# A hand-drawn issue order drawn anew: gated linear attention followed by a SoLU feed-forward block

## The chip, the core and the metric

The kernel runs on one NeuronCore of one Trainium2 chip. The metric is the device time of one execution in microseconds. The engines are called PE (TensorE matmul), PEld (its weight loads), DVE (VectorE), ACT (ScalarE), POOL (GpSimd) and SP (SyncE, whose queue issues most DMAs). Each engine works off its own queue in the order in which the program issues to it, so an instruction that waits holds up those behind it on its engine.

## The reference, cut to what matters

```python
# attention: q, k, v, alpha are (4, 8, 768, 48) float32, alpha in 0.8 .. 1.0
for t in range(S):
    state = alpha[:, :, t, :, None] * state + einsum('bhd,bhe->bhde', k[:, :, t], v[:, :, t])
    y[:, :, t] = einsum('bhd,bhde->bhe', q[:, :, t], state)
x = y.transpose(0, 2, 1, 3).reshape(3072, 384)
# feed-forward: w_in (384, 1024), w_out (1024, 384), both float64 in memory, g_ln (1024)
h = x @ w_in
solu = h * softmax(h)
ln = (solu - mean(solu)) / sqrt(var(solu) + 1e-6) * g_ln
out = ln @ w_out
```

## The kernel before, in words

**Tiling.** The 768 steps of a sequence are cut into G = 6 groups of 128. In a group all 4 batches and 8 heads are handled together: the batch gives a quarter of the 128 partitions. The output is made in N = 24 products of 128 tokens; product m belongs to group m // 4 and batch m % 4. "Product" below means the feed-forward work on 128 tokens.

**Attention of one group** is a chain over several engines:
- `load` (SP) brings alpha, k and q of a group into the tiles `an`, `kn`, `qn`, `load_v` brings v into `vn`. For group 0 `load_first` does it by token, and `turned` transposes on PE with `ends` copied by ACT first.
- `alpha_T` and `alpha_max` (DVE) transpose alpha and take its largest value.
- `scan_back(g, i)` (L179, DVE, a scan of 128x516, three thirds i) gives the decay hT; `keys_T` (L159 and L160, DVE transposes) and `keys` (L201, POOL) give the decayed keys kT; `decay` (L222, L225, POOL) decays the state.
- `scan_on(g, i)` (L189 to L193 and L179, DVE: copy, maximum, reciprocal, scan) gives the forward products in aT; `queries_T` (L159, L160) and `queries` (L213, L215, POOL) give the decayed queries qv; `apart` (L208, ACT) spreads the last columns of the queries by parity.
- `keys_back(g)` transposes kT on PE (L258) into PSUM banks, and ACT copies it to `kg` (L260).
- `scores(g, half)` (L239, PE, 64 instructions a half) fills four PSUM banks, and `masked(half)` (L250, DVE) multiplies them by the triangle mask into sT, which empties the banks.
- `read_begin`, `read_state` and `read_values` (L271, PE) make y; ACT copies it to xT (L296); `next_state` (L308 PE, L317 DVE) adds the group's state.

The four PSUM banks with the tags a0 to a3 are shared by the transposed keys, the scores, y and the state's product. Whoever comes next waits until the one before has been read.

**The feed-forward block of product m.** `up(m, half)`: 24 matmul instructions (L329) into one of two banks h, then on ACT e = exp(h) (L334), on DVE u = h e (L335), on ACT u squared (L336). The bank is free when u is made. `partial(m)` adds e on POOL and u squared on DVE over the eight column blocks (L344, L347, L349). `down(m, half)` is the product with w_out (L358), with two small sums (L364) at the end. `finish(m)` works out the scale (L373 to L380 DVE, `r` L384 POOL), ACT writes o_sb (L386), SP stores it (L388). The scale can only be made after the product is done, and o_sb frees one of two banks o.

**Conversion of the weights.** w_in and w_out come as float64 in 14 pieces: 0 to 5 are w_in (512 columns), 6 to 13 are w_out (384 columns). `fetch(i)` (L421, SP) loads a piece into one of four buffers `raw`; `bits(i)` (L437 to L444, four DVE instructions) splits it into `top` and `low`; `add(i)` adds the two on PE (L457, a product with the identity into a bank o) and ACT copies the sum into the weight (L461, L459); `in_range(i)` (L471, L474, ACT) tests the range and is the last reader of the buffer. `centre` subtracts the mean from w_out (L492 to L501), once all pieces are there.

**What sets the order.** The schedule is manual: the engines receive their instructions in the order of the calls at the end of the function. Ahead of the loop these calls are written out one by one: first the start, group 0 and products 0 to 3 with the conversions among them, then group 1 with the downs of products 0 to 3. In the loop over m from 4 to 24, product m rises (`up`), product m - 1 falls (`down`), product m - 2 is finished, and beside them the four steps s = 0 to 3 of group g = m // 4 + 1 are done, for g = 2 to 5.

Of the kernel before, what the change touches and what calls it, by code (L numbers as in the profile page):

```python
# [16 lines left out]
P = 128  # L17
# [15 lines left out]
def fast_path(ctx, tc, q, k, v, alpha, moe_w_in, moe_w_out, moe_g_ln, out):  # L33
# [104 lines left out]
    def turned(src, out):  # L138

        x = by_token(src)  # L140
        ends = two.tile([P, B, H * E1], FP, tag="two", name="ends")
        nc.scalar.copy(out=ends.rearrange("p b (h d) -> p b h d", h=H), in_=x[:, :, :, E0:D])
# [14 lines left out]
    def blocks(src, dst, extra):  # L157

        nc.vector.transpose(out=dst.rearrange("p h (t u) -> p h u t", u=TQ), in_=src[:, :, :, 0:E0])  # L159
        nc.vector.transpose(  # L160
            out=extra.rearrange("p j (i t u) -> p u j i t", u=TQ, i=2),
            in_=src[:, :, :, E0:D].rearrange("p (j i) u d -> p u j i d", i=2),
        )

# [38 lines left out]
    def queries_T(g):  # L203
        blocks(qn, qv[:, 0:H], qe)
# [7 lines left out]
    def queries(g):  # L212
        nc.gpsimd.tensor_tensor(out=qe, in0=qe, in1=aT[:, H:NB, 1:SW], op=ALU.mult)  # L213
        apart()
        nc.gpsimd.tensor_tensor(out=qv[:, 0:H], in0=qv[:, 0:H], in1=aT[:, 0:H, 1:SW], op=ALU.mult)  # L215
# [212 lines left out]

    def bits(i):
# [15 lines left out]
        made[i] = low, top.bitcast(FP)  # L445

# [15 lines left out]

    def in_range(i):


        if not float64:
            return
        F = words(i)[0].shape[1]
        raw = raws.pop(i)
        sq = work.tile([P, 512], FP, name="sq")[:, 0:F]  # L470
        nc.scalar.activation(  # L471
            out=sq, in_=raw[:, 0:F, 1].bitcast(FP), func=AF.Square, accum_out=far[:, i, 0:1]
        )
        nc.scalar.activation(out=sq, in_=sq, func=AF.Exp, scale=-(2.0**24), accum_out=far[:, i, 1:2])  # L474

    def convert(i):
        bits(i)
        add(i)
        in_range(i)
# [28 lines left out]

    nc.scalar.dma_start(out=ident, in_=inline(np.eye(P), "ident_c"))
    for i in range(3):  # L510
        fetch(i)
    load_first(alpha, an)
# [3 lines left out]
    nc.scalar.dma_start(out=g_rows, in_=moe_g_ln.rearrange("(c p) -> c p", p=P))  # L516
    load_first(k, kn)
    load_first(q, qn)
    nc.gpsimd.memset(unit, 0.0)
    nc.gpsimd.memset(unit[:, :, 0:1], 1.0)  # L520
    nc.gpsimd.memset(vn, 0.0)
# [8 lines left out]
    load_v(0)  # L530
    fetch(3)

    for i in range(3):
        bits(i)
        add(i)
    alpha_max(0)
    t = banks("tp_a", [NP, P], 3)
    turned(an, t)
    for i in range(3):
        nc.scalar.copy(out=aT[:, NP * i : NP * i + NP, 1:SW], in_=t[i])  # L540
    for i in range(3):
        in_range(i)
        fetch(i + 4)
        scan_back(0, i)
    t = [ps_h.tile([P, NP, P], FP, tag="h", name=f"tp_k{i}") for i in range(2)]
    t.append(ps_a.tile([P, NP, P], FP, tag="a3", name="tp_k2"))
    turned(kn, t)
# [4 lines left out]
    turned(qn, t)  # L552
# [10 lines left out]
    bits(3)  # L563
    masked(0)
    scores(0, 1)
    add(3)
    masked(1)
    bits(4)
    read_begin()
    read_values(0)  # L570
    add(4)
    for i in (3, 4):
        in_range(i)
        fetch(i + 4)
    load(alpha, an, 1)


    up(0, 0)
    up(1, 0)
    bits(5)  # L580
    add(5)
    keys_back(0)
    next_state(0)
    in_range(5)
    fetch(9)
    load(k, kn, 1)
    up(0, 1)
    convert(6)
    fetch(10)
    up(1, 1)  # L590
    partial(0)
    convert(7)
    fetch(11)
    partial(1)
    convert(8)
    fetch(12)
    up(2, 0)
    convert(9)
    fetch(13)
    load(q, qn, 1)  # L600
    load_v(1)
    up(2, 1)
    partial(2)
    convert(10)
    convert(11)
    up(3, 0)
    convert(12)
    convert(13)
    up(3, 1)
    centre()  # L610
# [3 lines left out]
    for i in range(3):  # L614
        scan_back(1, i)
    decay(1)
    down(0, 0)
    down(0, 1)
    keys_T(1)
    keys(1)  # L620
    finish(0)
    for i in range(3):
        scan_on(1, i)
    down(1, 0)
    down(1, 1)
    queries_T(1)
# [557 lines left out]
```

## Time and profile before

| | us |
|---|---|
| median of three runs | 556.03 (553.51 to 556.2) |
| the profiled execution's own time | 554.89 |
| its span, first to last instruction | 553.0 |
| PE busy | 435.9 (79%) |
| DVE busy | 273.3 (49%) |
| POOL busy | 140.6 (25%) |
| ACT busy | 130.5 (24%) |
| mean granted PE clock | 0.883 of full |

The page of the profile also follows the chain of work that ended last, from the last instruction back. By engine it reads:

```profile
PE 55%; DVE 28%; issue 5%; ACT 5%; POOL 3%; DMA 2%; SPq 0%; DVEq 0%; ACTq 0%
```

PE holds a little over half of the chain and DVE more than a quarter: the end is set by PE and DVE in turns. The groups of instructions show the largest shares of PE; the columns are busy time, mean ns of one instruction, and the idle time before them with its releaser:

```profile
L329 PE MATMUL h<-xT,w_in 128*128 128x128 f32 x1152 | 138.4, 280 | 0.0
L358 PE MATMUL o<-w_out,u 128*128 128x385 f32 x384 | 134.5, 500 | 1.1 <-DVE w_out L501 0.6
L239 PE MATMUL a<-qv,kT 32*128 32x128 f32 x768 | 51.6, 396 | 55.5 <-POOL qv L215 34.1
```

A mean of one instruction is longer than its share of the time, since matmuls overlap. Busy shares are averages over stages with different limits, so a change is read from its own stage.

### The profile page before, as it was taken

To read this page: it belongs to the slowest core of one execution; us is meant where nothing else is said; L and a number is where in the kernel's file an instruction comes from. 1 tells how busy PE (TensorE), PEld (TensorE's weight loads), DVE (VectorE), ACT (ScalarE), POOL (GpSimd) and SP (SyncE) were. 2 spreads that over 40 slices of the span, in tenths; PEclk is the share of its full clock that TensorE was granted. 3 is DMA by queue.
4 is the path that set the end of the run, shared out by engine and by line. 5 is a ranking of instruction groups with operands and counts; after the bars stand their busy time and mean duration, and the time that the engine had idled before them with its cause. 6 is when DMAs were issued, how large, how long until landed. Compare 5 with 4: busy or idle time off the path is not lost.

```text
span 553.0 us, 12123 instructions
## 1 busy us (share of the span) xinstructions
PE 435.9 (79%) x5365; PEld 345.1 (62%) x5365; DVE 273.3 (49%) x483; ACT 130.5 (24%) x252; POOL 140.6 (25%) x148
## 2 busy tenths in 40 slices
PE   4769755478669598389995699994899948999993
PEld 1558543345447496367884577884589736888772
DVE  4583335444973338444477245583542873313431
ACT  1603423233020032111222212231122221223220
POOL 3000021201420026222064302362220832202430
PEclk9878887879886899579998789996899988999997
DMA  6970441530003564012235130415213100000001
GB/s 161 177 160 6 113 112 57 99 45 0 0 30 78 110 101 88 0 32 43 41 48 107 22 72 19 58 32 112 58 32 44 31 15 0 17 18 15 14 17 49
DMA packets 85118, 30.90 MB, mean 56 GB/s; under 512 B 64568, under 2 KB 83264, under 8 KB 85056
## 3 DMA queue, kind: packets, MB, share of 16 engines
q1 hardware_dynamic: 84608, 29.90, 26.4%
q8 instruction: 44, 0.72, 0.6%
q10 hardware_dynamic: 448, 0.14, 0.1%
q14 instruction: 18, 0.15, 0.1%
HBM read 25.30 MB, written 4.72 MB: 54 GB/s over the span
## 4 chain that ended last, share of the span: by engine, by line
PE 55%; DVE 28%; issue 5%; ACT 5%; POOL 3%; DMA 2%; SPq 0%; DVEq 0%; ACTq 0%
PE h L329 18%; PE o L358 11%; PE a L239 8%; PE y L271 8%; PE sum L457 6%; DVE aT L179 3%; DVE hT L179 3%; DVE u L335 2%; DVE part_u L344 2%; DVE part_u L347 2%; ACT e L334 2%; ACT u L336 2%; DVE qv L159 2%; DVE kT L159 2%; DVE sT L250 2%
## 5 line engine op out<-in xcount | busy, mean ns | idle before, releaser
L329 PE MATMUL h<-xT,w_in 128*128 128x128 f32 x1152 | 138.4, 280 | 0.0
L329 PEld LDWEIGHTS h<-xT,w_in 128*128 128x128 f32 x1152 | 134.9, 196 | 5.1 <-issue 4.1
L358 PE MATMUL o<-w_out,u 128*128 128x385 f32 x384 | 134.5, 500 | 1.1 <-DVE w_out L501 0.6
L335 DVE TENSOR_TENSOR u<-h,e 128x512 f32<-128x512 f32 x48 | 33.2, 691 | 170.4 <-ACT e L334 170.4
L344 POOL TENSOR_TENSOR part_e<-e 128x512 f32<-128x512 f32 x24 | 30.6, 1273 | 292.3 <-ACT e L334 292.3
L358 PEld LDWEIGHTS o<-w_out,u 128*128 128x128 f32 x384 | 72.0, 194 | 49.0 <-issue 4.9
L239 PE MATMUL a<-qv,kT 32*128 32x128 f32 x768 | 51.6, 396 | 55.5 <-POOL qv L215 34.1
L239 PEld LDWEIGHTS a<-qv,kT 32*128 32x128 f32 x768 | 46.0, 294 | 61.8 <-POOL qv L215 34.8
L334 ACT ACTIVATE e<-h 128x512 f32<-128x512 f32 x48 | 28.5, 593 | 102.7 <-PE h L329 102.6
L457 PE MATMUL sum<-low,ident 128*128 128x384 f32 (+1 forms) x28 | 21.3, 858 | 35.4 <-DVE low L444 35.4
L336 ACT ACTIVATE u<-u 128x512 f32<-128x512 f32 x48 | 30.2, 630 | 48.7 <-DVE u L335 48.7
L250 DVE TENSOR_TENSOR sT<-a,mask 128x512 f32<-128x512 f32 x48 | 29.7, 680 | 21.3 <-PE a L239 21.3
L386 ACT ACTIVATE o_sb<-o,r 128x384 f32<-128x384 f32 x24 | 14.0, 582 | 109.7 <-POOL r L384 109.7
L457 PEld LDWEIGHTS sum<-low,ident 128*128 128x128 f32 x28 | 6.3, 265 | 41.1 <-DVE low L444 23.3
L384 POOL TENSOR_TENSOR r<-sums,mhalf 128x1 f32<-128x1 f32 x24 | 15.8, 660 | 54.7 <-DVE sums L380 54.6
L347 POOL TENSOR_TENSOR part_e<-part_e 128x256 f32<-128x256 f32 x24 | 28.3, 1181 | 1.9
L344 DVE TENSOR_TENSOR part_u<-u 128x512 f32<-128x512 f32 x24 | 19.0, 793 | 14.6 <-ACT u L336 14.6
L271 PE MATMUL y<-sT,vn 128*32 128x128 f32 x768 | 24.4, 290 | 0.0
L271 PE MATMUL y<-qv,state 32*32 32x128 f32 x1280 | 19.1, 281 | 5.8 <-issue 5.8
L271 PEld LDWEIGHTS y<-sT,vn 128*32 128x32 f32 x768 | 22.5, 118 | 1.5 <-issue 1.1
L296 ACT COPY xT<-y 128x384 f32<-128x384 f32 x24 | 11.5, 479 | 46.6 <-PE y L271 46.6
L179 DVE TENSOR_TENSOR_SCAN aT<-aT,seed 128x516 f32<-128x516 f32 x18 | 22.2, 1232 | 0.6
(101 smaller groups left out, 437.7 us busy)
## 6 DMA issues: line engine op xcount, KB each, us to landing
an<-in_alpha_dram SPq DMA_DIRECT2D x24, 192.0 KB, 4.1
kn<-in_k_dram SPq DMA_DIRECT2D x24, 192.0 KB, 5.0
qn<-in_q_dram SPq DMA_DIRECT2D x24, 192.0 KB, 4.5
out_dram<-o_sb SPq DMA_DIRECT2D x24, 192.0 KB, 1.9
vn<-in_v_dram SPq DMA_DIRECT2D x24, 128.0 KB, 3.4
raw<-in_moe_w_out_dram SPq DMA_DIRECT2D x8, 384.0 KB, 3.9
raw<-in_moe_w_in_dram SPq DMA_DIRECT2D x16, 128.0 KB, 3.2
vn<-in_v_dram SPq DMA_DIRECT2D x24, 64.0 KB, 3.1
```

Of the source, the lines that this page charges most:

```text
L179: nc.vector.tensor_tensor_scan(out=o, data0=a, data1=s, initial=1.0, op0=ALU.mult, op1=ALU.add)
L239: nc.tensor.matmul(a[b][:, i], lhsT=kT[quarter(b), kb], rhs=qv[quarter(b), qb], start=kb == h, stop=kb != h, tile_position=(32 * b, 0), sk ...
L250: nc.vector.tensor_tensor(out=sT[:, b, half * NP : half * NP + NP], in0=a[b], in1=mask[:, None, :].to_broadcast([P, NP, P]), op=ALU.mult,)
L271: nc.tensor.matmul(reading["y"][b][quarter(r), a], lhsT=lhsT, rhs=rhs, start=(b, r) not in begun, stop=stop, tile_position=(row, 32 * r), ...
L329: nc.tensor.matmul(h[:, f], lhsT=w_in[:, a, (f0 + f) * P : (f0 + f + 1) * P], rhs=d["xT"][:, a], start=(a == 0), stop=(a == KC - 1),)
L334: nc.scalar.activation(out=d["e"][:, fs], in_=h, func=AF.Exp)
L335: nc.vector.tensor_tensor(out=d["u"][:, fs], in0=h, in1=d["e"][:, fs], op=ALU.mult)
L336: nc.scalar.activation(out=d["u2"][:, fs], in_=d["u"][:, fs], func=AF.Square)
L344: eng.tensor_tensor(out=t, in0=d[key][:, 0:HF], in1=d[key][:, HF:FC], op=ALU.add)
L347: eng.tensor_tensor(out=t[:, 0:w], in0=t[:, 0:w], in1=t[:, w : 2 * w], op=ALU.add)
L358: nc.tensor.matmul(o[:, 0 : DM + 1], lhsT=d["u"][:, f], rhs=w_out[:, f], start=(f == 0), stop=(f == FC - 1), skip_group_check=True,)
L457: nc.tensor.matmul(src, lhsT=ident, rhs=x, start=k == 0, stop=k == 1)
```

## The change

The computation is the same; every instruction of the function is still there. What differs is the order of the calls, and with it the order on each engine. Line numbers after the change are some lines higher (L179 becomes L186, L258 becomes L264).

- **Start.** Alpha is fetched ahead of the weights, keys and queries ahead of piece 2. The copy `ends` is taken out of `turned` and issued earlier. The sums of pieces 0 to 2, which stood ahead of group 0, are spread among its steps.
- **Conversions.** `in_range(i)` is issued with `bits(i)`, and `fetch(i + 4)` right behind it. Each `bits(i)` stands one product ahead of its `add(i)`.
- **Group 1.** Keys and the forward scans come before `down(0)` is finished, `apart` behind `finish(1)`, the first scores between the halves of `down(3)`; the loads of group 2 are spread.
- **Loop.** Two of the three backward scans move up to the step's start, keys come before the decay, two of the three forward scans move into step 0. In step 1 the last scan and the queries come between the halves of `up`, and the smaller query transpose comes first. In step 2 both halves of the scores come later: the first behind the whole `up`, the second behind the whole `down`.

```diff
-    def turned(src, out):
+    def ends_of(src):
+        ends = two.tile([P, B, H * E1], FP, tag="two", name="ends")
+        nc.scalar.copy(out=ends.rearrange("p b (h d) -> p b h d", h=H), in_=by_token(src)[:, :, :, E0:D])
+        return ends
+
+    def turned(src, ends, out):
...
     def queries_T(g):
-        blocks(qn, qv[:, 0:H], qe)
+        blocks(qn, qv[:, 0:H], qe, True)
...
     def queries(g):
         nc.gpsimd.tensor_tensor(out=qe, in0=qe, in1=aT[:, H:NB, 1:SW], op=ALU.mult)
-        apart()
         nc.gpsimd.tensor_tensor(out=qv[:, 0:H], in0=qv[:, 0:H], in1=aT[:, 0:H, 1:SW], op=ALU.mult)
...
         made[i] = low, top.bitcast(FP)
+        in_range(i)
...
+    load_first(alpha, an)
     nc.scalar.dma_start(out=ident, in_=inline(np.eye(P), "ident_c"))
-    for i in range(3):
-        fetch(i)
-    load_first(alpha, an)
...
+    fetch(0)
+    fetch(1)
     load_first(k, kn)
     load_first(q, qn)
+    fetch(2)
+    nc.gpsimd.memset(vn, 0.0)
+    load_v(0)
+    fetch(3)
...
-    load_v(0)
-    fetch(3)
-
-    for i in range(3):
-        bits(i)
-        add(i)
+
+    t = banks("tp_a", [NP, P], 3)
+    turned(an, ends_of(an), t)
     alpha_max(0)
...
+    bits(6)
+    fetch(10)
+    up(0, 1)
+    bits(7)
+    fetch(11)
+    add(6)
+    partial(0)
+    up(1, 1)
+    add(7)
+    bits(8)
+    fetch(12)
+    partial(1)
...
-    up(0, 1)
-    convert(6)
-    fetch(10)
-    up(1, 1)
-    partial(0)
-    convert(7)
-    fetch(11)
-    partial(1)
...
     for i in range(3):
         scan_back(1, i)
+    keys_T(1)
+    keys(1)
     decay(1)
     down(0, 0)
     down(0, 1)
-    keys_T(1)
-    keys(1)
-    finish(0)
+    load(alpha, an, 2)
     for i in range(3):
         scan_on(1, i)
+    finish(0)
+    queries_T(1)
+    queries(1)
     down(1, 0)
     down(1, 1)
-    queries_T(1)
-    queries(1)
     finish(1)
-    keys_back(1)
+    apart()
+    load(k, kn, 2)
     down(2, 0)
     down(2, 1)
+    keys_back(1)
+    finish(2)
+    down(3, 0)
     scores(1, 0)
     masked(0)
-    finish(2)
+    load(q, qn, 2)
+    down(3, 1)
     scores(1, 1)
     masked(1)
...
+        if rise:
+            up(m, 0)
         if attn and s == 0:
             load_v(g)
-        if rise:
-            up(m, 0)
-        if attn and s == 2:
-            scores(g, 0)
+            scan_back(g, 0)
+            scan_back(g, 1)
+        elif attn and s == 1:
+            scan_on(g, 2)
+            queries_T(g)
+            queries(g)
         if rise:
             up(m, 1)
             partial(m)
-        if attn and s == 2:
+        if attn and s == 1:
+            apart()
+        elif attn and s == 2:
+            scores(g, 0)
             masked(0)
...
         if s == 0:
-            for i in range(3):
-                scan_back(g, i)
+            scan_back(g, 2)
             keys_T(g)
+            keys(g)
             decay(g)
-            keys(g)
+            scan_on(g, 0)
+            scan_on(g, 1)
         elif s == 1:
             keys_back(g)
-            for i in range(3):
-                scan_on(g, i)
-            queries_T(g)
-            queries(g)
             if more:
                 load(alpha, an, g + 1)
                 load(k, kn, g + 1)
         elif s == 2:
+            scores(g, 1)
+            masked(1)
             if more:
                 load(q, qn, g + 1)
```

Three places show what this does to the engines' queues. The first is DVE while the weights are converted, from the second half of product 0, `up(0, 1)`, on: u is `up`'s product, the rows with raw, top and low are the `bits` of piece 6. Before:

```order
L335 TENSOR_TENSOR u<-h,e 128x512
L437 TENSOR_SCALAR top<-raw 128x384
L440 SCALAR_TENSOR_TENSOR top<-raw,top 128x384
L443 TENSOR_SCALAR low<-top 128x384
L444 SCALAR_TENSOR_TENSOR low<-raw,low 128x384
L335 TENSOR_TENSOR u<-h,e 128x512
```

After, the same place:

```order
L456 TENSOR_SCALAR top<-raw 128x384
L459 SCALAR_TENSOR_TENSOR top<-raw,top 128x384
L462 TENSOR_SCALAR low<-top 128x384
L463 SCALAR_TENSOR_TENSOR low<-raw,low 128x384
L341 TENSOR_TENSOR u<-h,e 128x512
```

The four rows of piece 6 stood behind the u of product 0's second half; they now stand ahead of it, and those of piece 7 follow in its place.

The second is DVE in the loop, group 4, behind the key transposes (kT<-kn). u and part_u are the next product's, sums to t its predecessor's finish; fend, least, seed and the scan of aT are `scan_on`. Before:

```order
L159 STREAM_TRANSPOSE kT<-kn 128x8x4x32
L160 STREAM_TRANSPOSE kT<-kn 128x4x128
L335 TENSOR_TENSOR u<-h,e 128x512 x2
L344 TENSOR_TENSOR part_u_2967<-u_2929 128x512
L347 TENSOR_TENSOR part_u_2967<-part_u_2967 128x256
L349 TENSOR_TENSOR sum_u_2968<-part_u_2967 128x128
L373 COPY sums<-o 128x3
```

After:

```order
L170 STREAM_TRANSPOSE kT<-kn 128x8x4x32
L170 STREAM_TRANSPOSE kT<-kn 128x4x128
L196 COPY fend<-hT 128x4
L199 TENSOR_SCALAR least<-hT 128x4
L200 RECIPROCAL seed_108<-least 128x4
L186 SCALAR_TENSOR_TENSOR aT<-aT,seed_108 128x516
L196 COPY fend<-hT 128x4
L199 TENSOR_SCALAR least<-hT 128x4
L200 RECIPROCAL seed_109<-least 128x4
L186 SCALAR_TENSOR_TENSOR aT<-aT,seed_109 128x516
L341 TENSOR_TENSOR u<-h,e 128x512
```

Two forward scans have moved ahead of the next product's first u; the third and the query transposes follow directly behind that u, and its partial sum and finish come after them.

The third is PE in the same group, from the transposes of the keys (tp) to the first scores (a, four banks). Before:

```order
L258 MATMUL tp_2996<-ident,kT 128x128 x4
L329 MATMUL h<-xT,w_in 128x128 x12
L239 MATMUL a_3060<-qv,kT 128x128
L239 MATMUL a_3061<-qv,kT 128x128
L239 MATMUL a_3062<-qv,kT 128x128
```

After:

```order
L264 MATMUL tp_3017<-ident,kT 128x128 x4
L335 MATMUL h<-xT,w_in 128x128 x24
L245 MATMUL a_3086<-qv,kT 128x128
L245 MATMUL a_3087<-qv,kT 128x128
L245 MATMUL a_3088<-qv,kT 128x128
```

One half of `up` stood between the transposes and the first scores; now both halves do. (A row's x12 counts calls; the profile counts two instructions to each.)

122 lines of the change are left out of this document (60 added, 62 removed).

## The prediction

> **What bounds the kernel now.** I read first the table of stretches, cut where products start: from, to and length, then busy time (instructions) of TensorE, weight loads, VectorE, ScalarE and GpSimd, then the granted clock, DMA share and GB/s.
>
> ```profile
> 0.00:68.40 68.40, 47.50 (x726) 35.44 (x726) 34.32 (x61) 23.10 (x49) 5.12 (x12) 0.88 0.59 124
> 68.40:133.20 64.80, 40.26 (x198) 27.97 (x194) 25.70 (x49) 21.92 (x55) 11.05 (x13) 0.82 0.33 67
> 133.20:197.90 64.70, 47.35 (x701) 36.19 (x701) 40.34 (x61) 6.93 (x13) 11.93 (x12) 0.82 0.22 47
> 197.90:272.40 74.50, 60.59 (x877) 51.05 (x873) 39.21 (x60) 15.45 (x27) 22.79 (x22) 0.86 0.27 52
> 272.40:347.20 74.80, 64.39 (x897) 52.67 (x893) 40.31 (x68) 16.62 (x29) 24.72 (x24) 0.91 0.28 54
> 347.20:422.20 75.00, 64.57 (x897) 52.77 (x893) 40.35 (x68) 16.62 (x29) 24.73 (x24) 0.91 0.28 54
> 422.20:493.70 71.50, 61.08 (x796) 49.91 (x796) 35.14 (x64) 16.13 (x28) 24.66 (x23) 0.93 0.13 23
> ```
>
> I call the first three rows A (start, first up products), B (weight conversion beside products) and C (from the centred w_out to product 4); the next four are the loop's groups g=2 to 5; a tail without attention follows. No engine fills A, B or C. In the groups TensorE leads, yet it waits. The waits of TensorE say for what (total, times, longest):
>
> ```profile
> PE sum L457 <- DVE low L444: 35.4, 8, 8.3
> PE a L239 <- POOL qv L215: 34.1, 4, 10.8
> PE a L239 <- DVE sT L250: 9.7, 6, 2.2
> PE y L271 <- issue: 5.8, 1, 5.8
> ```
>
> The conversion sums wait 35.4 us for VectorE's bit work, mostly in B. The scores wait once per group for the queries (34.1) and for a bank that masking empties (9.7). TensorE's timeline of g=4 (start, length, idle before in brackets) shows both, and what a group costs without them:
>
> ```profile
> 347.16 5.62 PE L329 MATMUL h<-xT,w_in 128*128 128x128 f32 x48
> 352.62 5.35 PE L358 MATMUL o<-w_out,u 128*128 128x385 f32 x16
> 358.17 5.61 PE L329 MATMUL h<-xT,w_in 128*128 128x128 f32 x48
> 369.16 1.51 PE L258 MATMUL tp<-ident,kT 128*128 128x128 f32 x12
> 381.12 3.80 PE L239 MATMUL a<-qv,kT 32*128 32x128 f32 x64 [7.78 <-POOL qv L215]
> 393.16 4.35 PE L239 MATMUL a<-qv,kT 32*128 32x128 f32 x64 [2.22 <-DVE sT L250]
> 407.12 1.90 PE L271 MATMUL y<-qv,state 32*32 32x128 f32 x128
> 416.70 3.70 PE L271 MATMUL y<-sT,vn 128*32 128x128 f32 x128
> 422.10 1.16 PE L329 MATMUL h<-xT,w_in 128*128 128x128 f32 x8
> ```
>
> A product (up and down) is 369.16 - 358.17 = 11.0, its up 5.46. Four products are 44.0, the transposes 1.5, two state reads 3.8, values with the state's product 422.10 - 416.70 = 5.4. Half of a group's scores takes 3.8, but at half clock, as the next fence shows. At full clock no row has it alone: 1.9 (all of it halved) to 3.8; I take 2.7, between, since the weight loads do not all follow the clock. Dense, a group is 44.0 + 1.5 + 3.8 + 5.4 + 5.4 = 60.1, against 75.0.
>
> The clock is the rest. The table of stretches again, cut behind the two waits:
>
> ```profile
> 381.10:386.00 4.90, 4.88 (x69) 4.65 (x70) 0.41 (x1) 0.63 (x1) 0.00 (x0) 0.50 0.00 0
> 396.20:399.60 3.40, 3.40 (x29) 2.26 (x23) 2.41 (x4) 0.50 (x1) 0.00 (x0) 0.51 0.52 151
> ```
>
> Each wait is paid twice: the clock is 0.50 for the 4.9 us behind the long one, and 0.51 again from 396.2, behind the 2.22 one.
>
> **A: the start.** Alpha, keys and queries now pass weight transfers on SyncE's queue.
>
> ```profile
> 0.74 9.34 SPq L421 DMA_DIRECT2D raw<-in_moe_w_in_dram  x16
> 51.53 1.02 PE L457 MATMUL sum<-top,ident 128*128 128x512 f32 x2
> ```
>
> One issue is 9.34/16 = 0.58 us. Alpha passes 16, but keys and queries only 8 (pieces 0 and 1 stay ahead), and the scores hang on the queries: 8 x 0.58 = 4.7 earlier. The sum of piece 4 leaves the path between the values and the first product: two pairs like the row, about 1.9. A: -6.6, bounded by -9.3 (all 16 passed) and 0 (the transfers, at 124 GB/s over A, arrive no sooner).
>
> **B: conversions.** The groups of instructions, for this stretch alone (busy, mean ns, idle before and its releaser), put most of the sums' waits here:
>
> ```profile
> L457 PE MATMUL sum<-low,ident 128*128 128x384 f32 x16 | 12.0, 853 | 23.5 <-DVE low L444 23.5
> ```
>
> The bit work of a piece is now issued ahead of the product before its sum, so these 23.5 go, and with them the cold clock that made a 384-column instruction 853 ns. TensorE's own work becomes the bound: six half products of 2.73 are 16.4, eight sums of 384 columns, each three quarters of two pairs like the 1.02 row, 8 x 1.53 = 12.2, centring about 3: 31.6. VectorE (25.7) and ScalarE (21.9) lie beside it. Their order still binds at the end, where the last two pieces, ScalarE's copies and the mean follow each other: I add 3.5. B is 35.1: -29.7; at worst 64.8 stays. The fetches move with it: a piece's buffer is free only after its range check, and q, k and v now stand behind the last fetch; at 67 GB/s over B, against 124 over A, there is room for the same bytes in half the time.
>
> **C: the group 1 hand-over.** From the timeline and, cut finer, the table of stretches:
>
> ```profile
> 184.00:186.00 2.00, 0.00 (x0) 0.00 (x0) 1.90 (x5) 0.00 (x0) 0.00 (x0) 1.00 1.14 209
> 153.00 5.88 PE L358 MATMUL o<-w_out,u 128*128 128x385 f32 x16
> 190.22 5.94 PE L271 MATMUL y<-sT,vn 128*32 128x128 f32 x128
> ```
>
> The 5.8 issue wait of the y matmuls lies beside the loads of group 2, all issued at once: the DMA share is 1.14 while TensorE does nothing. In the new order they are spread over C, so I drop the wait, and the values then take 3.70, not 5.94 (-2.2). Half of down(3), 2.8, fills part of the wait for the scores. Against that, finish(0) goes behind three scans, so the down(2) of the row at 153.00 starts some 5 later; all but 1.8 was idle anyway. C: -5.8 - 2.2 - 2.8 + 1.8 = -9.0, between -10.8 (finish(0) costs nothing) and 0 (the issue wait and its cold clock stay, and finish(0) costs its whole 5).
>
> **The groups.** The queries' chain moves a product up. What is late next? VectorE, ScalarE and GpSimd in g=4:
>
> ```profile
> 350.83 0.69 DVE L335 TENSOR_TENSOR u<-h,e 128x512 f32<-128x512 f32 x1 [2.77 <-ACT e L334]
> 354.84 0.69 DVE L344 TENSOR_TENSOR part_u<-u 128x512 f32<-128x512 f32 x1 [0.70 <-ACT u L336]
> 357.43 3.47 DVE L179 TENSOR_TENSOR_SCAN hT<-aT,unit 128x516 f32<-128x516 f32 x3
> 360.82 2.07 DVE L159 STREAM_TRANSPOSE kT<-kn 128x1024 f32<-128x1024 f32 x1
> 363.67 0.69 DVE L335 TENSOR_TENSOR u<-h,e 128x512 f32<-128x512 f32 x1
> 370.46 1.23 DVE L179 TENSOR_TENSOR_SCAN aT<-aT,seed 128x516 f32<-128x516 f32 x1
> 372.07 1.23 DVE L179 TENSOR_TENSOR_SCAN aT<-aT,seed 128x516 f32<-128x516 f32 x1
> 357.59 1.41 POOL L384 TENSOR_TENSOR r<-sums,mhalf 128x1 f32<-128x1 f32 x1 [0.88 <-DVE sums L380]
> 370.13 0.55 POOL L384 TENSOR_TENSOR r<-sums,mhalf 128x1 f32<-128x1 f32 x1 [0.88 <-DVE sums L380]
> 362.97 3.33 POOL L201 TENSOR_TENSOR kT<-kT,hT 128x1024 f32<-128x1024 f32 x2
> 378.90 2.17 POOL L215 TENSOR_TENSOR qv<-qv,aT 128x1024 f32<-128x1024 f32 x1
> 371.20 1.55 ACT L260 COPY kg<-tp 128x512 f32<-128x512 f32 x3
> ```
>
> Count from a group's first matmul. VectorE's first u starts at 3.7. Then, in the new order: two u with the square between them 2.1, two scans back 2.3, partial sum and finish 2.6 (354.84 to 357.43), third scan 1.16, key transposes 2.85 (360.82 to 363.67): 14.7. Two scans on at 1.61 and the late u bring 18.6, the third and the query transposes 23.1. GpSimd multiplies the keys meanwhile, and a scan and a GpSimd operation exclude each other: r takes 1.41 beside a scan, 0.55 alone. Alternating costs VectorE some 2 us: 25. Then qv to 27.3, and VectorE's partial sum alternates with GpSimd's, some 3.4; finish 0.7, r 0.55, o_sb 0.6, and only then ScalarE copies the transposed keys (1.55), which frees the banks of the scores: 32.7 to 34.0. TensorE wants them at 11.0 + 11.0 + 1.5 + 5.46 = 29.0. So the wait moves from the queries to the key copies; I take 4.5, between 2.4 (no exclusion) and the present 10. The second scores stand behind a whole down (5.5), longer than masking needs, so the 2.22 goes. Cold clock: one half at 3.8 instead of 2.7, and the 4.9 - 3.8 = 1.1 left at half clock cost about 0.6. A group: 60.1 + 4.5 + 1.1 + 0.6 = 66.3.
>
> The Trainium skill, page "SBUF — State Buffer", section "Who interferes with whom", makes the port pair that VectorE and GpSimd share an exclusive lock, taken also by a VectorE instruction with two SBUF inputs; r, 1.41 against 0.55, agrees. Without that lock the sum would be about 6 us lower.
>
> For g=2, which has no down in its first step: 60.1 - 5.5 + 1.7 and a wait of 6.5, as VectorE has less cover there: 62.8. For g=5, which has no state product (some 1.9 of the 5.4): 64.4. Gains: 74.5 - 62.8 = 11.7, then 8.5, 8.7, 7.1: -36.0, between -62.8 (dense) and 0. The tail's order is the same: 0.
>
> **Sum.** -6.6 - 29.7 - 9.0 - 36.0 = -81.3. The profiled execution took 554.9 (span 553.0, 1.9 around it), 0.2% under the median of 556.0: 554.9 - 81.3 = **474**.
>
> **Rivals.** *Dense groups* (0.13): the key copies come before TensorE asks. For it: no other engine has over 40.4 us of work in a group. Against it: finish stands behind the query transposes. 474 - 26.8 = 447. The Trainium skill's "TensorE: Matmul & The Clock Gate" (Part 1) halves the clock after an idle window of about 3.4 us; by it a wait cut to 2.4 would leave the clock up and most of this case would come. The 2.22 wait, shorter than that, had 0.51 behind it all the same.
>
> *The lead does not hold in B* (0.08): the four raw buffers and ScalarE's in-order range checks hold the bit work back as before; the change then does not do what it says. 474 + 29.7 = 504.
>
> *The wait only moves in the loop* (0.10): VectorE falls a product behind and groups stay at 74.8. 474 + 36.0 = 510.
>
> *Slower* (0.03): the heads of the queues lock the helpers into strict turns, in the groups VectorE, ScalarE and GpSimd (40.31 + 16.62 + 24.72 = 81.7 for 74.8; 316.7 for 295.8 over the four), in B also TensorE (87.9 for 64.8). 554.9 + 20.9 + 23.1 = 599. It turns the sign once B and the groups, 360.6 now, pass 360.6 + 15.6 (gains of A and C) = 376.2 of their 404.6 in turns; now they overlap.
>
> **How the numbers follow.** The forecast has 0.66, own range 456 to 493. With the dense case and the edge of the case B the range is 446 to 500; about 0.2 lies outside. Half a per cent, 2.8 us, is about what a measurement here can tell from no change: faster 0.95, same 0.02, slower 0.03.
>
> **What would show it.** A: the first scores some 4.7 earlier. B: no 4 us waits of the sums, 35 long. C: no issue wait. Groups: no wait for qv, one of 2 to 6 us of the first scores for the key copies (kg), none for sT. Wrong if u of the second product holds up TensorE's up, or if the sums still wait for the low words.

## The result and the profile after

The changed kernel takes 471.18 us (median of four runs, 469.6 to 472.39) against 555.68 before (four runs, 553.51 to 556.2) measured beside it: a ratio of 0.848, with a 95% interval of 0.845 to 0.852. The forecast was 474 with a range of 446 to 500. The profiled execution spans 470.6 us, 82.4 less than the 553.0 before.

Where the time went is read from the table of stretches of the changed kernel, cut at the same events as before (the start of the third half product `up(0,1)`, the first subtraction of the mean from `w_out`, `up(4,0)`, and the first product of each later group). Columns: from, to and length; busy time (instructions) of TensorE, weight loads, VectorE, ScalarE, GpSimd; granted clock, DMA share, GB/s.

```profile
0.00:57.53 57.53, 46.07 (x725) 34.81 (x726) 35.63 (x65) 22.71 (x49) 5.11 (x12) 0.91 0.72 155
57.53:92.26 34.73, 30.22 (x195) 22.84 (x193) 24.56 (x46) 21.01 (x54) 10.38 (x13) 1.00 0.56 114
92.26:151.57 59.31, 42.45 (x700) 29.81 (x700) 40.71 (x61) 6.91 (x13) 12.96 (x12) 0.86 0.24 55
151.57:212.43 60.86, 56.91 (x874) 47.80 (x872) 43.12 (x60) 15.24 (x27) 23.70 (x22) 0.97 0.31 60
212.43:279.80 67.37, 62.99 (x897) 51.94 (x893) 44.58 (x68) 16.41 (x29) 25.72 (x24) 0.95 0.31 60
279.80:345.97 66.17, 61.80 (x897) 51.03 (x893) 44.57 (x68) 16.41 (x29) 25.72 (x24) 0.97 0.32 61
345.97:411.35 65.38, 61.01 (x800) 50.11 (x796) 39.37 (x64) 15.93 (x28) 25.64 (x23) 0.95 0.14 26
```

Row by row against the rows of before:

| stretch | before | after | difference | forecast |
|---|---|---|---|---|
| A | 68.40 | 57.53 | -10.9 | -6.6 |
| B | 64.80 | 34.73 | -30.1 | -29.7 |
| C | 64.70 | 59.31 | -5.4 | -9.0 |
| groups g=2 to 5 | 295.80 | 259.78 | -36.0 | -36.0 |
| tail | 59.3 | 59.25 | 0.0 | 0 |

The sum is right to 1.1 us, and it is so partly by luck: A gave more than was forecast and C less. The waits of TensorE (total, times, longest) show which waits are gone and which are new:

```profile
PE o L364 <- ACT o_sb L392: 14.2, 2, 13.7
PE a L245 <- ACT kg L266: 12.2, 3, 4.1
PE h L335 <- DVE u L341: 4.2, 5, 2.8
PE sum L477 <- DVE low L463: 3.3, 4, 1.0
PE y L277 <- issue: 1.2, 2, 0.6
```

The sums wait 3.3 us for VectorE's bit work instead of 35.4; the wait for `qv` (34.1) isn't among them any more; the masks cost 0.4 in front of the scores instead of 9.7. New are a single wait of 13.7 for `o_sb`, in C, and three of 4.1 for the key copies `kg`, one in each of g=3 to 5. TensorE's timeline of g=4 shows what such a wait costs (start, length, operation, and in brackets the idle time before it with its releaser):

```profile
301.81 1.51 PE L264 MATMUL tp<-ident,kT 128*128 128x128 f32 x12
306.29 2.94 PE L335 MATMUL h<-xT,w_in 128*128 128x128 f32 x24 [0.30 <-DVE u L341]
313.31 4.46 PE L245 MATMUL a<-qv,kT 32*128 32x128 f32 x64 [4.08 <-ACT kg L266]
323.43 2.07 PE L245 MATMUL a<-qv,kT 32*128 32x128 f32 x64
```

The transposes `tp` are done at 303.3, and yet the scores wait until 313.3 for their copies. The second half of the scores takes 2.07 us, the first, behind the wait, 4.46. The stretch table over most of the first shows a granted clock of 0.59:

```profile
313.50:317.70 4.20, 4.20 (x64) 3.76 (x63) 1.38 (x2) 2.69 (x6) 1.11 (x1) 0.59 0.87 205
```

Such a half, at a clock far below full, is called cold from here on. VectorE, GpSimd and ScalarE in the same 10 us, each on its own timeline, say why the copies are late:

```profile
306.93 1.59 DVE L350 TENSOR_TENSOR part_u<-u 128x512 f32<-128x512 f32 x1 [0.70 <-ACT u L342]
308.56 1.37 DVE L353 TENSOR_TENSOR part_u<-part_u 128x256 f32<-128x256 f32 x1
309.96 0.69 DVE L355 TENSOR_TENSOR sum_u<-part_u 128x128 f32<-128x128 f32 x1
307.93 1.72 POOL L350 TENSOR_TENSOR part_e<-e 128x512 f32<-128x512 f32 x1
311.53 0.55 POOL L390 TENSOR_TENSOR r<-sums,mhalf 128x1 f32<-128x1 f32 x1 [0.48 <-DVE sums L386]
312.11 0.58 ACT L392 ACTIVATE o_sb<-o,r 128x384 f32<-128x384 f32 x1 [3.99 <-POOL r L390]
312.59 1.55 ACT L266 COPY kg<-tp 128x512 f32<-128x512 f32 x3
```

ScalarE sits idle for 3.99 us with the copies next but one in its queue: it waits for `r`, which comes from GpSimd behind its partial sum, and needs `sums` from VectorE, whose own partial sum takes 1.59 + 1.37 + 0.69 beside GpSimd's `qv` (up to 307.98) and partial sum.

### The profile page after: what moved, and what is told of

It is laid out like the page before. It is cut to its first block, busy times and chain, and to the rows that moved or that the text cites. A ratio compares the mean times of both kernels' runs of the same rounds, so it can differ in the third digit from the quotient of the medians.

```text
span 470.6 us, 12126 instructions
## 1 busy us (share of the span) xinstructions
PE 411.6 (87%) x5365; PEld 327.4 (70%) x5365; DVE 290.5 (62%) x483; ACT 128.4 (27%) x252; POOL 144.8 (31%) x148
## 4 chain that ended last, share of the span: by engine, by line
PE 52%; DVE 31%; ACT 5%; issue 5%; SPq 3%; DMA 2%; POOL 1%; DVEq 0%; ACTq 0%
PE o L364 16%; PE h L335 14%; PE y L277 9%; PE a L245 7%; DVE aT L186 4%; DVE kT L170 3%; DVE part_u L350 3%; DVE u L341 3%; DVE fend L196 3%; DVE hT L186 3%; DVE part_u L353 2%; PE kv L314 2%; SPq L136 2%; ACT u L342 2%; DVE qv L170 2%
## 5 line engine op out<-in xcount | busy, mean ns | idle before, releaser
L350 POOL TENSOR_TENSOR part_e<-e 128x512 f32<-128x512 f32 x24 | 32.6, 1358 | 220.1 <-ACT e L340 220.1
L342 ACT ACTIVATE u<-u 128x512 f32<-128x512 f32 x48 | 30.2, 630 | 84.2 <-DVE u L341 84.2
L245 PE MATMUL a<-qv,kT 32*128 32x128 f32 x768 | 39.2, 339 | 15.9 <-ACT kg L266 12.2
L245 PEld LDWEIGHTS a<-qv,kT 32*128 32x128 f32 x768 | 35.5, 242 | 18.7 <-issue 16.6
L350 DVE TENSOR_TENSOR part_u<-u 128x512 f32<-128x512 f32 x24 | 22.0, 915 | 13.9 <-ACT u L342 13.9
L186 DVE TENSOR_TENSOR_SCAN aT<-aT,seed 128x516 f32<-128x516 f32 x18 | 25.9, 1436 | 0.6
L353 POOL TENSOR_TENSOR part_e<-part_e 128x256 f32<-128x256 f32 x24 | 24.3, 1012 | 1.9
L208 POOL TENSOR_TENSOR kT<-kT,hT 128x1024 f32<-128x1024 f32 (+1 forms) x10 | 16.6, 1679 | 26.3 <-DVE kT L170 26.3
L277 PE MATMUL y<-qv,state 32*32 32x128 f32 x1280 | 21.3, 297 | 2.0 <-DVE sT L256 1.4
L277 PEld LDWEIGHTS y<-qv,state 32*32 32x32 f32 x1280 | 16.5, 107 | 7.2 <-issue 3.1
L186 DVE TENSOR_TENSOR_SCAN hT<-aT,unit 128x516 f32<-128x516 f32 x18 | 21.2, 1218 | 0.0
```

The lines of the kernel that those rows point to most:

```text
L186: nc.vector.tensor_tensor_scan(out=o, data0=a, data1=s, initial=1.0, op0=ALU.mult, op1=ALU.add)
L245: nc.tensor.matmul(a[b][:, i], lhsT=kT[quarter(b), kb], rhs=qv[quarter(b), qb], start=kb == h, stop=kb != h, tile_position=(32 * b, 0), sk ...
L277: nc.tensor.matmul(reading["y"][b][quarter(r), a], lhsT=lhsT, rhs=rhs, start=(b, r) not in begun, stop=stop, tile_position=(row, 32 * r), ...
L342: nc.scalar.activation(out=d["u2"][:, fs], in_=d["u"][:, fs], func=AF.Square)
L350: eng.tensor_tensor(out=t, in0=d[key][:, 0:HF], in1=d[key][:, HF:FC], op=ALU.add)
L353: eng.tensor_tensor(out=t[:, 0:w], in0=t[:, 0:w], in1=t[:, w : 2 * w], op=ALU.add)
```

## The experiments

Twelve kernels were run. The first nine of the table change one thing each (start_only and loop_only keep one half of the change); the last three put edits together. Each was timed against the kernel before on the same chip; before took 552.7 to 555.2 in these groups of runs.

| run | us, median | ratio to before, 95% interval |
|---|---|---|
| changed kernel | 471.2 | 0.848 (0.845 to 0.852) |
| start_only | 506.2 | 0.914 (0.910 to 0.917) |
| loop_only | 516.3 | 0.933 (0.929 to 0.937) |
| no_lead | 525.0 | 0.949 (0.944 to 0.953) |
| old_fetch_order | 476.6 | 0.859 (0.855 to 0.862) |
| scores_close | 478.7 | 0.864 (0.860 to 0.868) |
| keys_copied_first | 466.7 | 0.842 (0.839 to 0.846) |
| gpsimd_half_late | 464.9 | 0.838 (0.835 to 0.842) |
| finish0_first | 469.5 | 0.846 (0.841 to 0.850) |
| loads_together | 475.6 | 0.859 (0.854 to 0.864) |
| loop_combined | 450.8 | 0.816 (0.812 to 0.819) |
| all_combined | 444.3 | 0.805 (0.802 to 0.809) |
| decay_late | 439.5 | 0.795 (0.791 to 0.799) |

### The two halves apart: start_only and loop_only

start_only keeps the new order up to `next_state(1)` and has the old body of the loop; loop_only the other way round.

> The new order ahead of the loop (stretches A, B and C), the old order in the loop. Theory, the two halves are independent: A, B and C give 197.9 - 151.6 = 46.3 us by the two profiles, so 555.7 - 46.3 = 509, and the loop's groups keep their old 74 to 75 us with the waits for qv. Rival, the loop's gain or loss depends on how late the start hands over its queries and keys: more than 5 us away from 509.

> The old order ahead of the loop, the new order in the loop. Theory, independent halves: the groups g=2 to 5 give 295.8 - 259.8 = 36.0 us, so 555.7 - 36 = 520, with one wait of some 4.1 us for kg in each of g=3 to 5. Rival, part of the loop's gain needs the new start: over 525.

Before took 553.7 beside them: start_only gave 47.5 us, loop_only 37.5, together 85.0, where the whole change gives 84.5 by its own comparison. The halves are independent to within what is measured here. The waits of TensorE say the same, first those of start_only:

```profile
PE a L245 <- POOL qv L712: 34.1, 4, 10.8
```

and those of loop_only, whose lines are numbered a little lower:

```profile
PE sum L461 <- DVE low L448: 35.6, 8, 8.4
PE a L243 <- ACT kg L264: 12.3, 3, 4.1
PE y L275 <- issue: 5.8, 1, 5.8
PE a L243 <- issue: 5.3, 1, 5.3
```

With the old loop the wait for the queries is back to the tenth (34.1); with the old start the sums' wait (35.6) and two issue waits (5.8 and 5.3) are back, and the loop still has its three waits for `kg`. The second issue wait, ahead of the scores, was there before the change too, and the prediction priced only the first:

```profile
PE a L239 <- issue: 5.4, 1, 5.4
```

### Without the lead: no_lead

```diff
-    bits(6)
-    fetch(10)
+    fetch(9)
     up(0, 1)
-    bits(7)
-    fetch(11)
+    bits(6)
     add(6)
+    fetch(10)
     partial(0)
     up(1, 1)
+    bits(7)
     add(7)
-    bits(8)
-    fetch(12)
+    fetch(11)
```

The same for every piece from 0 to 13.

> The changed kernel, with the bit work of each of the 14 pieces (and the fetch behind it) put back right ahead of its sum; all else stays. Theory, the lead is what took the waits of the sums out of B: they come back (23 us and more in waits, cold sums), 471 + 30 = 501. Rival, the gain of B came from the other moves (the loads of q, k and v behind the last fetch, the products between the sums): 480 or less.

It took 525.0, 54 over the changed kernel and more than either theory said. The waits of the sums are back, 24.6 us of them in B:

```profile
PE sum L477 <- DVE low L463: 39.8, 11, 4.5
```

The table of stretches of no_lead, cut at `up(0,1)` and at the first subtraction:

```profile
0.00:78.49 78.49, 52.46 (x726) 37.91 (x726) 35.15 (x62) 23.42 (x49) 5.11 (x12) 0.85 0.53 111
78.49:145.87 67.38, 41.85 (x195) 29.50 (x193) 26.66 (x47) 22.26 (x54) 10.85 (x13) 0.80 0.32 62
```

B is 67.4 instead of 34.7, 32.7 more: the lead (the bit work and the fetch behind it, moved together here) is the gain of B, and the forecast of -29.7 was its size. The other 21.0 are in A, 78.5 for 57.5: there the kernel before had a lead as well (the bit work of pieces 0 to 2 at the very start, of 3 ahead of the first masks), which this experiment takes away too. That part of it undoes more than the change did.

### The order of the first transfers: old_fetch_order

```diff
-    load_first(alpha, an)
     nc.scalar.dma_start(out=ident, in_=inline(np.eye(P), "ident_c"))
+    for i in range(3):
+        fetch(i)
+    load_first(alpha, an)
...
-    fetch(0)
-    fetch(1)
     load_first(k, kn)
     load_first(q, qn)
-    fetch(2)
-    nc.gpsimd.memset(vn, 0.0)
-    load_v(0)
-    fetch(3)
...
+    nc.gpsimd.memset(vn, 0.0)
...
+    load_v(0)
+    fetch(3)
```

> The changed kernel with the transfers of the start in their old order (identity and three pieces ahead of alpha; keys, queries, then values and piece 3), everything else new. Theory, the load order gives the 4.7 us that were forecast for it and the rest of A's 10.9 comes from the order of the sums: 471 + 4.7 = 476. First rival, the bytes arrive no sooner and the order of issue gives nothing: 472 or less. Second rival, it gives all of the 7.3 us by which the first scores come earlier, or more, since the tail of the start hangs on it: 478 or more.

476.6, which is 5.4 over the changed kernel and near the first theory in total. But the path isn't the one that the theory names. Two rows of its TensorE timeline:

```profile
12.91 1.35 PE L149 MATMUL tp_a<-ident,an 128*32 128x128 f32 x4 [12.91 <-DMA an<-in_alpha_dram]
64.84 0.61 PE L335 MATMUL h<-xT,w_in 128*128 128x128 f32 x4
```

TensorE stands until 12.9 for alpha, and A ends at 64.84, 7.3 after the changed kernel's 57.53. By these profiles the order of the transfers carries 7.3 of A's 10.9, and the order of the sums the other 3.6 (68.40 - 64.84). Each is good to about 2 us only: in the ten profiles that share the new start A ends between 55.94 and 58.10, and in the two with the old start at 68.40 and 66.40 (loop_only). The rest of the program gave some 1.9 of the 7.3 back. B is as long as in the changed kernel (34.7); C is 57.7 for 59.3, with the `down(2)` behind its long wait in 6.85 for 7.84 and the long read of the state in 3.14 for 4.33.

### The second scores close to the first: scores_close

```diff
         if fall:
             down(m - 1, 0)
+        if attn and s == 2:
+            scores(g, 1)
+            masked(1)
...
         elif s == 2:
-            scores(g, 1)
-            masked(1)
```

> The changed kernel with the second half of a group's scores put back between the two halves of down, one half product behind the first. Theory, a half down of 2.8 us doesn't cover the masking: a wait of some 2.2 us for sT comes back in each of the four groups, and a cold half of scores (4.4 instead of 2.07): 471 + 4 x 4.5 = 489. Rival, the masks now come in time, since the first half starts late by the wait for kg: 474 or less.

478.7: 7.5 over the changed kernel, between the two. The wait for `sT` came back in g=2 alone (2.05). In g=3 to 5 there is none, but the second half takes longer, as in its g=4:

```profile
320.23 2.86 PE L364 MATMUL o<-w_out,u 128*128 128x385 f32 x8
323.16 3.84 PE L245 MATMUL a<-qv,kT 32*128 32x128 f32 x64
```
Over the second of them the stretch table has:

```profile
323.10:327.00 3.90, 3.49 (x65) 2.80 (x65) 2.49 (x9) 0.58 (x1) 0.55 (x1) 1.00 0.46 85
```

The clock is 1.00, so it isn't cold. VectorE is still masking the first half, until 324.8, and frees the four banks one after another: the weight loads of the second half wait for `sT` three more times, 0.3 us each. 3.84 - 2.07 = 1.8 in each of three groups and some 2.9 in g=2 (2.05 of wait, and 3.84 against the 3.02 of the changed kernel) are 8.2, the measured amount within the runs' spread. Moving the scores down a product is worth this much; my theory had the wrong price, a cold half, for most of it.

### The key copies ahead of o_sb: keys_copied_first

```diff
-        if m > B + 1:
+        if m > B + 1 and not (attn and s == 1):
             finish(m - 2)
...
             keys_back(g)
+            if m > B + 1:
+                finish(m - 2)
```

> The changed kernel, with finish(m-2) of the loop's second step issued behind the transposes of the keys and their three copies, so that on ScalarE the copies no longer stand behind o_sb; no other engine's order in that step changes. Theory, the copies are late only because o_sb stands ahead of them: the three waits of 4.1 us go, and with them the cold half of scores (4.46 to 2.07) and up to 1 us of the following down, some 6.5 us in each of g=3 to 5: 471 - 19.5 = 452. Rival, another wait takes the place of this one (the queries' parity copies, the masks, or a buffer of o): at most a third of that, 464 or more.

466.7: 4.5 faster, not 19.5. The waits for `kg` are gone, as the theory said, and something took their place, as the rival said. The same place of g=4 in its timeline of TensorE:

```profile
305.90 2.51 PE L245 MATMUL a<-qv,kT 32*128 32x128 f32 x64
309.49 5.45 PE L364 MATMUL o<-w_out,u 128*128 128x385 f32 x16 [1.08 <-ACT o_sb L392]
315.89 5.44 PE L245 MATMUL a<-qv,kT 32*128 32x128 f32 x64 [0.61 <-DVE sT L256]
```
and the row of the stretch table over the second scores:

```profile
317.70:321.30 3.60, 3.60 (x59) 3.38 (x59) 0.79 (x4) 0.58 (x1) 0.55 (x1) 0.53 0.58 126
```

The first scores now run without a wait in 2.51. But `down` then waits 1.08 for the buffer that `o_sb` empties, and the second scores 0.61 for the masks. The masks free the banks one after another, so that only 9 of the 64 instructions fall in the next 1.8 us, still at a clock of 1.00; from 317.7 on the clock is at 0.53. The cold half has only moved to the second scores (5.44 instead of 2.07).

### GpSimd's partial sum behind r: gpsimd_half_late

```diff
-            partial(m)
+            partial(m, (1,) if attn and s == 1 else (0, 1))
...
         if m > B + 1:
             finish(m - 2)
+        if attn and s == 1:
+            partial(m, (0,))
```

(0 is GpSimd's sum of `e`, 1 VectorE's of `u2`.)

> The changed kernel; in the loop's second step GpSimd's partial sum of e is issued behind finish, so that VectorE's partial sum of u and finish run beside less of GpSimd's work. Theory, the two engines exclude each other: VectorE's three instructions go from 1.59 + 1.37 + 0.69 = 3.65 to about 1.4, or 1.9 beside the end of qv, r and o_sb come some 2 us earlier and the wait for kg falls from 4.1 to about 2: 471 - 3 x 2.1 = 465. Rival, they don't exclude each other and the 3.65 stay: 470 or more.

464.9, as the theory said, though the wait fell from 4.08 to 2.59 and not to 2. VectorE's three instructions in its g=4:

```profile
302.80 1.60 DVE L350 TENSOR_TENSOR part_u<-u 128x512 f32<-128x512 f32 x1 [0.70 <-ACT u L342]
304.43 0.42 DVE L353 TENSOR_TENSOR part_u<-part_u 128x256 f32<-128x256 f32 x1
304.89 0.29 DVE L355 TENSOR_TENSOR sum_u<-part_u 128x128 f32<-128x128 f32 x1
```
and the scores behind them on TensorE:

```profile
307.69 3.93 PE L245 MATMUL a<-qv,kT 32*128 32x128 f32 x64 [2.59 <-POOL part_e L350]
```
with the row of the stretch table over most of them, at a clock of 0.75:

```profile
307.70:311.10 3.40, 3.40 (x62) 3.07 (x64) 0.86 (x2) 2.44 (x5) 1.31 (x3) 0.75 0.81 201
```

The first still runs beside GpSimd's `qv`; the second and third go from 1.37 and 0.69 to 0.42 and 0.29. (Here the releaser shown is `part_e`; the copies of `kg` still end last, behind `o_sb`.) The Trainium skill, page "SBUF — State Buffer", section "Who interferes with whom", calls the port pair that the two engines share an exclusive lock; these rows agree.

### finish(0) ahead of the scans: finish0_first

```diff
         scan_back(1, i)
+    down(0, 0)
+    down(0, 1)
+    finish(0)
     keys_T(1)
     keys(1)
     decay(1)
-    down(0, 0)
-    down(0, 1)
...
-    finish(0)
```

> The changed kernel, with finish(0) put ahead of the transposes of group 1's keys and of the three scans, directly behind down(0). Theory, the 13.7 us wait of down(2) for o_sb is a cost of the new order: down(2) starts at some 104 instead of 118, the next to be late are the queries' parity copies (end 123.3 instead of 124.6, scores at 130.1 so far), so the first scores come up to 6.8 earlier, less some 2.4 for a cold half: 471 - 4.4 = 467. Rival, VectorE's and GpSimd's chain to the queries sets the end of C and the wait only moves behind down(2), to the scores: 470 or more.

469.5, 1.7 faster: between the two, and not clear of the changed kernel by the intervals. Two rows of its C:

```profile
107.22 8.51 PE L364 MATMUL o<-w_out,u 128*128 128x385 f32 x16 [2.89 <-ACT o_sb L392]
123.50 4.62 PE L364 MATMUL o<-w_out,u 128*128 128x385 f32 x8 [6.06 <-ACT o_sb L392]
```

The wait of 13.7 shrank to 2.9, and 6.1 of it came back one product later: `finish(1)` still stood behind the queries, as it had before the change.

### The loads of group 2 together again: loads_together

```diff
-    load(alpha, an, 2)
...
-    load(k, kn, 2)
...
-    load(q, qn, 2)
...
+    load(alpha, an, 2)
+    load(k, kn, 2)
+    load(q, qn, 2)
     read_begin()
```

> The changed kernel, with the loads of group 2's alpha, keys and queries issued together ahead of the reads, as before the change. Theory (the prediction's), TensorE's issue wait of 5.8 us in the y matmuls came of these transfers bunched beside them: the wait comes back in the y matmuls, with the values cold behind it (5.9 instead of 3.7): 471 + 5.8 + 2.2 = 479, less the 1.2 of short issue waits that are there now, 478. Rival, it came of where the other work stood (what TensorE does in the 30 us ahead of it) and not of the loads: no issue wait over 1.5 us, 473 or less.

475.6, 4.4 slower. Issue waits are back, in the values and in the first product of group 2, not all where they were before, on the timeline of TensorE:

```profile
148.01 0.96 PE L277 MATMUL y<-sT,vn 128*32 128x128 f32 x26 [1.64 <-issue]
155.31 4.91 PE L335 MATMUL h<-xT,w_in 128*128 128x128 f32 x28 [3.82 <-issue]
```
The stretch table shows what stands beside the longest:

```profile
152.00:154.00 2.00, 0.00 (x0) 0.00 (x0) 2.00 (x3) 0.00 (x0) 0.00 (x0) 1.00 1.21 205
```

1.64 + 3.82 and a first one of 0.37 are 5.8, the amount of before, beside a DMA share of 1.21. The changed kernel has 1.7 (1.2, and 0.5 in the first product of group 2). That the bunched loads make TensorE wait is shown, and the 4.1 more are most of the 4.4. The cold values are not: they took 3.03 + 0.96 here as well. Alpha also arrives later, so the rest may be VectorE's.

### Put together: loop_combined, all_combined, decay_late

loop_combined has the two edits of the loop's second step and one of its third:

```diff
-            partial(m)
+            if not (attn and s == 2):
+                partial(m, (1,) if attn and s == 1 else (0, 1))
...
             scores(g, 0)
             masked(0)
+            partial(m)
...
-        if m > B + 1:
+        if m > B + 1 and not (attn and s == 1):
             finish(m - 2)
...
             keys_back(g)
+            if m > B + 1:
+                finish(m - 2)
+            partial(m, (0,))
```

> The changed kernel with three edits in the loop: in the second step the key copies ahead of finish and GpSimd's partial sum behind both; in the third step the first masks ahead of the partial sums. Theory, the two single edits gained only some 4.5 and 6 us because each left one short wait (o_sb 1.08 and sT 0.61; kg 2.6) and behind it a half of scores at half clock; with none of these waits left, groups 3 to 5 come near the dense 60.1, 61 with the small wait for u: 471 - (67.4 + 66.2 + 65.4 - 3 x 61) = 455. Rival, the halves of scores lose the clock without a wait, or another wait comes up: groups stay at 64 or more, 463 or more.

450.8, 20.4 us under the changed kernel, where the two edits of the second step gave 4.5 and 6.3 alone: each had left one or two short waits standing, and the clock went with them. The third edit, the masks of the third step, has no run of its own, so how the 20.4 divide among the three isn't shown.

all_combined also moves, ahead of the loop:

```diff
+    down(0, 0)
+    down(0, 1)
+    finish(0)
+    down(1, 0)
+    down(1, 1)
+    finish(1)
     keys_T(1)
...
-    down(0, 0)
-    down(0, 1)
...
-    finish(0)
...
-    down(1, 0)
-    down(1, 1)
-    finish(1)
```

> The kernel loop_combined, and ahead of the loop finish(0) and finish(1) directly behind their down products, ahead of group 1's key transposes. Theory, in finish0_first the wait of 13.7 became 2.9 and 6.1 since finish(1) still stood behind the queries; with both ahead, down(2), the transposes and half of down(3) run without a wait and the scores wait only for the queries' parity copies at some 124.6 instead of 130.1, less a cold half of 2.4: 3 to 5 us under loop_combined, 451 by the forecast for it. Rival, VectorE's chain is made later by the two finishes and sets the end of C: within 1.5 us of loop_combined.

444.3, 6.6 under loop_combined, more than the 3 to 5 expected. The longest wait in C is now 5.83, of the scores for `qv`.

decay_late moves GpSimd's decay of the state:

```diff
-    decay(1)
...
     queries(1)
+    decay(1)
...
             keys(g)
-            decay(g)
...
             scores(g, 1)
             masked(1)
+            decay(g)
```

> The kernel all_combined, with GpSimd's decay of the state (4.1 us a group) taken from beside the scans and put behind the queries ahead of the loop, and behind the second scores in the loop. Theory, GpSimd's instructions hold up VectorE's short copies and scans: the second and third fend copies go from 0.95 and 0.5 to 0.16, the scan from 1.32 to 1.23, about 1 us less in VectorE's chain of each group; ahead of the loop, where that chain sets the end of C, it is 1 to 1.5 us under all_combined, in the loop nothing waits for it any more. Rival, the decay then holds up the masks behind the second scores: slower than all_combined.

439.5, the fastest, 4.7 under all_combined: more than expected. Two copies ahead of the forward scans in its g=4, on VectorE's timeline:

```profile
277.97 1.57 DVE L196 COPY fend<-hT 128x4 f32<-128x4 f32 x1
281.67 0.14 DVE L196 COPY fend<-hT 128x4 f32<-128x4 f32 x1
```
The stretch of g=3 in all_combined:

```profile
202.61:262.67 60.06, 59.75 (x896) 49.19 (x892) 42.48 (x68) 16.39 (x29) 24.69 (x24) 1.00 0.34 68
```
and in decay_late:

```profile
204.33:263.48 59.15, 59.15 (x896) 48.93 (x893) 41.63 (x69) 16.40 (x29) 22.82 (x24) 1.00 0.34 69
```

The first copy still runs beside GpSimd's keys, the second, which stood beside the decay and took 0.96 at this place of the changed kernel, takes 0.14. I had said that nothing in the loop would wait for this chain; a wait of 0.29 for `u` was left in each group, and it goes: TensorE is busy for all of the 59.15, at full clock. 0.9 a group for three groups is 2.7 of the 4.7. The gain of 1 to 1.5 forecast for C is not in its length. Its scores do wait less for `qv`, 4.53 for 5.83, but C as a whole takes 52.4 for 52.6, at a clock of 0.90 for 0.94, and g=2 takes 0.4 more. The other 2.0 of the medians are not placed; they are of the size by which A differs between executions of the same start.

## Why the prediction was right, and where not

**A: -10.9 for -6.6.** The term for the transfers was mis-sized. It counted the eight issues that keys and queries pass, 4.7, since the scores hang on the queries. old_fetch_order shows some 7 (6.7 to 8.9 by the spread of A): alpha, which passes 16 issues, had TensorE standing until 12.9 there, and all that follows starts with it. That leaves 1.6 to 3.6 for the sums taken off the path, where 1.9 was forecast, so this term isn't shown to be wrong. The bound of -9.3 was too tight: it has the 16 issues alone, without the 1.9 of the sums that the forecast adds to them.

**B: -30.1 for -29.7.** Right, for the reason given: without the lead B is 67.4. Its length, 34.7, is close to the 35.1 forecast, but its parts offset each other: TensorE's own work is 30.2 for 31.6, and its idle time of 4.5 is 2.4 of short waits for the low words and 1.8 at the end, where a drain of 3.5 was expected. "If the sums still wait for the low words" was named as a sign of being wrong; they do, but for 1.0 at most.

**C: -5.4 for -9.0.** The step that failed is "finish(0) goes behind three scans, so the down(2) of the row at 153.00 starts some 5 later; all but 1.8 was idle anyway". The issue waits did go (5.8 and 5.4 before, 1.2 after), and loads_together shows what brings such waits. But TensorE's idle time in C is what it was: 64.70 - 47.35 = 17.4 before, 59.31 - 42.45 = 16.9 after. The wait for `o_sb`, 13.7 in one piece, took the place of the issue waits; what C gained is busy time at a better clock (0.82 to 0.86). `down(2)` starts 25.8 us into C where it had started 19.8, and on one wait alone. With both finishes ahead of the forward scans 6.6 more are to be had. For `finish(0)` alone 1.8 was near the mark (1.7 by the medians, which is not clear of no change, and 2.7 by the length of C in the two profiles): the mistake was to look at it alone, while `finish(1)` stayed behind the queries.

**Groups: -36.0 for -36.0.** The main step, that the wait moves from the queries to the key copies because `finish` stands ahead of them on ScalarE, was right, and its size too: 4.1 for 4.5, in g=3 to 5. (The first scores of g=4 start 33.5 into the group, at 313.31; the copies were forecast for 32.7 to 34.0.) Its cause is shown by two edits that act on it in different ways, keys_copied_first and gpsimd_half_late. Two terms around it were off and cancelled: a dense group is 59.2, not 60.1 (half of the scores takes 2.07 at full clock, not 2.7), and the cold clock costs 2.4 on the first half of the scores alone, not 1.1 + 0.6. In g=2 the step was wrong: no wait for `kg`, but 2.8 for `u` of the second product, behind the scans, which the prediction had named as a sign against itself. Its own reason could not hold there: in that step of g=2 (m = 5) the loop issues no `finish`, so no `o_sb` stands ahead of the copies. g=2 took 60.9 for 62.8.

**The rivals.** That the lead doesn't hold in B and that the loop's wait stays as long fell with the result. Dense groups did not come by the change, and the reason given against them, that finish comes late, held as long as the key copies stood behind it on ScalarE; in loop_combined they stand ahead of it, and a group takes 60.05. For that rival a rule was weighed by which a wait cut to 2.4 would leave the clock up. It doesn't hold in these runs: gpsimd_half_late has 2.59 of wait and a clock of 0.75 behind it, keys_copied_first two waits of 1.08 and 0.61, 1.8 us of few matmuls and then a clock of 0.53. The rule is in the Trainium skill, "TensorE: Matmul & The Clock Gate" (Part 1), an idle window of about 3.4 us; none of these waits is so long. The price of the rival *Slower*, 599, is short of its own rule: its 87.9 for B are TensorE, VectorE and ScalarE, and with GpSimd's 11.05 the turns there would take 98.9.

## What to carry to other kernels

When a wait is removed, look down the in-order queue of the engine that now comes last: here an unrelated output copy stood ahead of the key copies, and one swap on ScalarE, which changes no other engine's order in that step, took the wait away. Remove short waits together: one edit that left another wait of 1 us, or of 2.6, gained 4.5 or 6.3 us, the two together with a third 20. And when a step moves behind a long chain, ask the same of every later step that shares its buffers, not of that one alone.

## What the runs showed of the hardware

- **VectorE and GpSimd take turns, but not in every instruction.** A copy of four elements a partition takes 0.14 us alone and up to 1.57 beside GpSimd (decay_late). GpSimd's decay takes 1.98 and some 2.1 beside VectorE's scans, and 1.06 and 1.21 beside the masks, which read PSUM and keep their 2.48 (decay_late, in the loop). Ahead of the loop two small steps of VectorE's finish still waited for the queries and the decay (2.02 and 0.98 for 0.16 each).
- **The clock fell behind waits of 1 to 2.6 us, but not behind each.** It was 0.75 behind the 2.59 of gpsimd_half_late, and 0.53 in keys_copied_first behind waits of 1.08 and 0.61 and 1.8 us of few matmuls. Behind the 2.05 of scores_close, in g=2, it was 1.00. In all_combined, with only 0.29 of wait in each of g=3 to 5, it stayed 1.00. How much idle time in which stretch decides it stays open.
- **Transfers can stop TensorE without a semaphore.** Issue waits of 5.8 us in all came and went with three bunched loads (DMA share 1.14 to 1.21). What holds TensorE during them no run shows.
